# Gate and up of a decode MLP summed with the contraction block outermost, and the last block of W_up loaded on its own

## The chip, the cores and the metric

The kernel runs on one core of a Trainium2 chip. The metric is the device time of one execution in microseconds (us); medians of several runs are quoted, with the lowest and the highest. The profile's span, counted from the program's first instruction to its last, is about 1.8 us shorter than the time.

## The reference

One decode step for two sequences (B = 2, one token, D = 512): layer norm, attention of 32 heads over a cache of 8192 keys and values of 128 elements, output projection and residual, then a second layer norm and a gated MLP with F = 1376:

```python
h  = x + attention(layernorm(x), k_cache, v_cache, wq, wo)
n  = layernorm(h)
gate = n @ W_gate          # 512 x 1376
up   = n @ W_up            # 512 x 1376
gate = gate * (gate > 0)
h2 = h + (gate * up) @ W_down   # 1376 x 512
```

Nearly all of the 281 MB that have to be read are the key and value caches. W_gate, W_up and W_down are 1376 KB each, and they come last.

## The kernel before

The MLP works on transposed vectors: the weights are the stationary operand of TensorE (loaded into it), and the two tokens are the moving one. `F` is cut into 11 chunks `fc` (ten of 128 and one of 96), the contraction `D` into `KC = 4` blocks of 128.

All weights of the tail lie in one tile `W` and are loaded through SyncE's queue, behind the last values:

```python
load_v(N - 1, CUTS)                                  # the last head group's V, in four parts
for g, w in enumerate((B_W_gate, B_W_up)):           # 1376 KB each
    nc.sync.dma_start(out=wgu[:, g], in_=w.rearrange("(c p) n -> p c n", p=P))
wd_l = misc.tile([P, D], bf16)
blocks = [(f, min(4, NF - f)) for f in range(0, NF, 4)]   # chunks 0-3, 4-7, 8-9
for f, r in blocks:                                  # 512, 512 and 256 KB
    nc.sync.dma_start(out=wd_sb[:, f:f + r, :]..., in_=B_W_down[f * P:(f + r) * P, :]...)
nc.sync.dma_start(out=wd_l[0:LASTW, :], in_=B_W_down[FULL:F, :])   # the last 96 rows
```

The sums of gate and up have the chunk outermost, so each chunk's four contraction blocks follow each other, and the first chunk already needs the last block:

```python
def mlp_in(g, ps):
    for fc in [NF] + list(range(NF)):        # the chunk of 96 first
        for c in range(KC):
            # lhsT: the 128 x 128 (or 128 x 96) weights of block c, chunk fc
            nc.tensor.matmul(out=ps[0:w, fc, :], lhsT=lhsT, rhs=hd[:, c, :],
                             start=(c == 0), stop=(c == KC - 1))
mlp_in(0, gate_ps)
var = variance(hd_f, "ln2")
mlp_in(1, up_ps)
# ... gate = max(gate_ps, 0) * 1/(var + eps); act = gate * up_ps, on VectorE, in two parts each
for fc in range(FC):                          # 44 matmuls, chunk by chunk
    for c in range(KC):
        nc.tensor.matmul(out=y_ps[:, c, :], lhsT=(wd_sb[:, fc] or wd_l)[:, c * P:(c + 1) * P],
                         rhs=act[0:w, fc, :], ...)
# ... y = y_ps + hc, two transposes, two copies, one store
```

The softmax here doesn't subtract the row's maximum and nothing guards it: scores larger than these inputs give would overflow.

## Time and profile before

| | before |
|---|---|
| time, median of 3 | 663.18 us (663.14 to 663.24) |
| span | 661.4 us |
| data read | 281 MB at 425 GB/s, DMA over 90% busy in 39 of 40 slices |
| up's matmuls | 654.24 to 655.95 |
| W_down's matmuls | 656.28 to 657.99 |

The page of before, three of its lines: the span, the busy time of each engine, and what the DMA engines moved.

```profile
span 661.4 us, 4234 instructions
...
PE 296.9 (45%) x1704; PEld 131.9 (20%) x1704; DVE 603.0 (91%) x244; ACT 85.0 (13%) x329; POOL 4.7 (1%) x19
...
DMA packets 10699, 281.32 MB, mean 425 GB/s; under 512 B 980, under 2 KB 1592, under 8 KB 4024
```

VectorE and the DMA engines are both above 90%. For a change at the very end of the kernel these shares say nothing; the end has to be read by itself. The timeline gives it. Its columns are start and length in us, engine, source line, operation, what it writes and reads, the number of instructions merged, and in brackets how long the engine sat idle before and what ended that.

```profile
650.84 1.63 PE L429 MATMUL gate_ps<-hd,W 128*96 128x2 bf16 x44 [0.25 <-DVE hd L415]
...
654.24 1.71 PE L429 MATMUL up_ps<-hd,W 128*96 128x2 bf16 x44 [1.34 <-DMA W<-in_B_W_up_dram]
...
655.99 0.24 DVE L448 TENSOR_TENSOR act<-gate,up_ps 96x2 bf16<-96x2 f32 x2 [2.42 <-PE up_ps L429]
656.28 1.61 PE L455 MATMUL y_ps<-act,W 128*128 128x2 bf16 x40 [0.33 <-DVE act L448]
...
657.75 0.24 PE L455 MATMUL y_ps<-act,wd_l 96*128 96x2 bf16 x4
```

TensorE waits 1.34 us for W_up, then sums up (44 matmuls), VectorE multiplies, and TensorE goes on with W_down. Seen in this way, an earlier start of up would move everything behind it. The view of waits (who waited for whom: total us, times, longest) says the same, and it names no wait of `y_ps` for W_down:

```profile
DVE act L448 <- PE up_ps L429: 2.4, 1, 2.4
...
PE up_ps L429 <- DMA W<-in_B_W_up_dram: 1.3, 1, 1.3
...
PE y_ps L455 <- DVE act L448: 0.3, 1, 0.3
```

The chain of waits, which goes from the last instruction back to whatever released each step, tells another story (start, length, what):

```profile
643.88 12.97 DMA W<-in_B_W_down_dram
...
656.90 0.59 PE y_ps L455 x16
...
657.51 0.49 PE y_ps L455 x12
...
658.03 0.18 DVE y L460
```

The chain does not pass through up at all. The matmuls of W_down's second block start at 656.90, and what released them is the landing of a W_down transfer at 656.85. A start that comes at the earliest moment its data allow can be held by these data even if the waits view lists nothing: each matmul is drawn 165 ns long while its successor starts after 27 ns, so the 0.22 us from matmul 16's start (656.681) to matmul 17's (656.900) leave only some 0.05 us of drawn idle time, and that is not listed.

The windows show the queue draining (in each line: busy time of PE, PEld, DVE, ACT, POOL, then the granted TensorE clock, the share of the DMA engines that is busy, and GB/s):

```profile
655.00:656.00 1.00, 0.95 (x32) 0.89 (x30) 0.01 (x1) 0.00 (x0) 0.00 (x0) 0.50 0.56 203
656.00:657.00 1.00, 0.67 (x19) 0.58 (x19) 0.23 (x2) 0.00 (x0) 0.00 (x0) 0.50 0.23 85
657.00:658.00 1.00, 0.97 (x28) 0.80 (x27) 0.00 (x0) 0.00 (x0) 0.00 (x0) 0.50 0.01 5
```

When a transfer has landed is a matter of its slowest engine. The Trainium skill ("DMA: Bandwidth & Descriptors", section "Why a DMA increments its semaphore by 16 and not by 1") says that a transfer runs on up to 16 DMA engines that finish independently and are counted by the semaphore, and that only the full 16 means that all data has landed. The trace has sixteen updates for each of the transfers below, and they lie up to 3.7 us apart at the end of this kernel. From the trace's records of semaphore updates (us):

```
before                 first engine   last engine
W_gate                       647.21        650.67
W_up                         650.64        654.20
W_down chunks 0-3            651.93        655.47
W_down chunks 4-7            653.21        656.85
W_down chunks 8-9            653.91        657.47
W_down last 96 rows          654.24        657.67
```

### The profile page before, as it was taken

How to read it: one execution, taken by the hardware profiler on the slowest of the kernel's cores; microseconds unless marked ns; L12 is line 12 of the kernel's file. 1: busy time of each engine (PE TensorE's matmuls, PEld its weight loads, DVE VectorE, ACT ScalarE, POOL GpSimd, SP SyncE). 2: the span in 40 equal slices, each digit the busy share in tenths (PEclk: the TensorE clock that was granted, in tenths of full speed). 3: DMA queues.
4: the chain of work that ended last, by engine and by line, in shares of the span. 5: the costliest groups of instructions: out<-in, count | busy, mean ns of one | idle time of the engine just before them, and what ended most of it. 6: DMA issues, size and time to landing. Idle time of an engine off the chain costs nothing.

```text
span 661.4 us, 4234 instructions
## 1 busy us (share of the span) xinstructions
PE 296.9 (45%) x1704; PEld 131.9 (20%) x1704; DVE 603.0 (91%) x244; ACT 85.0 (13%) x329; POOL 4.7 (1%) x19
## 2 busy tenths in 40 slices
PE   3108245090633708254380915637081552844346
PEld 1003112030211303122140301213030120321245
DVE  1698999999999999999999999999989999999991
ACT  2111101111100111110111110111111101111110
POOL 2000000000000000000000000000000000000000
PEclk9757768586775857777595867759586775866755
DMA  9999999999999999999999999999999999999996
GB/s 381 444 444 411 458 398 446 428 449 440 402 439 432 444 416 457 408 434 438 417 460 410 428 455 414 446 424 445 412 434 438 427 458 400 440 422 438 412 409 253
DMA packets 10699, 281.32 MB, mean 425 GB/s; under 512 B 980, under 2 KB 1592, under 8 KB 4024
## 3 DMA queue, kind: packets, MB, share of 16 engines
q1 hardware_dynamic: 10676, 281.06, 99.0%
q8 instruction: 13, 0.21, 0.1%
q14 instruction: 6, 0.05, 0.0%
q10 hardware_dynamic: 4, 0.00, 0.0%
HBM read 281.05 MB, written 0.00 MB: 425 GB/s over the span
## 4 chain that ended last, share of the span: by engine, by line
DVE 45%; DMA 41%; PE 8%; SPq 3%; ACT 2%; issue 1%; DVEq 0%
DMA kv<-in_A_k_cache_dram 34%; DVE kv L209 21%; DVE kv L202 21%; PE o L251 7%; DMA W<-in_A_wo_dram 3%; DVE sc L217 3%; SPq L375 3%; DMA W<-in_B_W_down_dram 2%; DMA wq_sb<-in_A_wq_dram 2%; ACT pm L234 2%; PE qps L164 1%; DVE ou L285 0%; DVE rep L282 0%; PE y_ps L455 0%; PE yt_ps L466 0%
## 5 line engine op out<-in xcount | busy, mean ns | idle before, releaser
L251 PE MATMUL o<-kv,pm 128*16 128x512 bf16 x960 | 250.6, 427 | 320.8 <-DMA kv<-in_A_v_cache_dram 290.6
L202 DVE TENSOR_TENSOR kv<-kv,qrep 128x16384 bf16<-128x16384 bf16 (+2 forms) x33 | 278.1, 8427 | 29.7 <-DMA kv<-in_A_k_cache_dram 29.5
L209 DVE TENSOR_TENSOR kv<-kv 128x8192 bf16<-128x8192 bf16 (+5 forms) x132 | 276.9, 2098 | 4.4
L251 PEld LDWEIGHTS <-pm 128*16 128x16 bf16 x960 | 92.4, 98 | 474.6 <-issue 299.4
L234 ACT ACTIVATE pm<-sc 32x128 bf16<-32x128 f32 (+1 forms) x128 | 61.6, 481 | 425.2 <-DVE sc L217 423.8
L217 DVE TENSOR_REDUCE sc<-kv 128x128 f32<-128x1024 bf16 (+2 forms) x33 | 39.2, 1188 | 3.3
L234 ACT ACTIVATION_READ_ACCUMULATOR pm<-sc 32x1 f32 x128 | 31.8, 248 | 0.0
L261 ACT ACTIVATE osb<-o,turn_of 16x128 f32<-16x128 f32 x60 | 16.6, 347 | 115.1 <-PE o L251 107.9
L275 PE MATMUL rep<-osb,head_of 16*128 16x128 f32 x112 | 17.2, 292 | 7.2 <-ACT osb L261 7.2
L275 PEld LDWEIGHTS rep<-osb,head_of 16*128 16x128 f32 x112 | 14.5, 183 | 14.2 <-ACT osb L261 13.1
L292 PE MATMUL o_b<-pm,kv 128*128 128x4 bf16 x256 | 7.4, 166 | 6.6 <-DMA kv<-in_A_v_cache_dram 6.6
L292 PEld LDWEIGHTS <-kv 128*128 128x128 bf16 x256 | 7.3, 105 | 6.9 <-DMA kv<-in_A_v_cache_dram 6.9
L385 PE MATMUL a_ps<-oc,W 128*128 128x2 bf16 x112 | 3.1, 165 | 12.1 <-DVE oc L313 12.1
L164 PE MATMUL qps<-wq_sb,xnb 128*32 128x512 bf16 x64 | 5.4, 501 | 4.8 <-DMA wq_sb<-in_A_wq_dram 4.8
L385 PEld LDWEIGHTS <-W 128*128 128x128 bf16 x128 | 3.7, 104 | 12.4 <-DMA W<-in_A_wo_dram 7.8
L164 PEld LDWEIGHTS <-xnb 128*32 128x32 bf16 x64 | 2.6, 116 | 7.2 <-issue 5.7
L429 PEld LDWEIGHTS <-W 128*128 128x128 bf16 (+1 forms) x88 | 3.3, 120 | 1.6 <-DMA W<-in_B_W_up_dram 1.4
L170 ACT ACTIVATE qrep<-qps 128x512 bf16<-128x512 f32 x4 | 2.4, 597 | 6.2 <-PE qps L164 6.2
L318 DVE RECIPROCAL zil<-zb 128x4 f32<-128x4 f32 x2 | 0.4, 178 | 2.9 <-PE zb L297 2.9
L137 PE MATMUL x_ps<-ident,x_row 2*128 2x2 bf16 x4 | 0.4, 172 | 5.4 <-DMA x_row<-in_A_x_dram 5.4
L285 DVE TENSOR_REDUCE ou<-rep 128x16 f32<-128x512 f32 (+1 forms) x4 | 2.5, 624 | 0.1
L282 DVE TENSOR_TENSOR rep<-rep,pick 128x512 f32<-128x512 f32 (+1 forms) x4 | 2.5, 626 | 0.0
(82 smaller groups left out, 38.9 us busy)
## 6 DMA issues: line engine op xcount, KB each, us to landing
kv<-in_A_k_cache_dram SPq DMA_DIRECT2D x32, 4096.0 KB, 32.3
kv<-in_A_v_cache_dram SPq DMA_DIRECT2D x3, 4096.0 KB, 25.0
wq_sb<-in_A_wq_dram SPq DMA_DIRECT2D x1, 4096.0 KB, 12.2
W<-in_A_wo_dram SPq DMA_DIRECT2D x1, 3584.0 KB, 21.1
kv<-in_A_v_cache_dram SPq DMA_DIRECT2D x1, 2560.0 KB, 26.0
W<-in_B_W_gate_dram SPq DMA_DIRECT2D x1, 1376.0 KB, 29.5
W<-in_B_W_up_dram SPq DMA_DIRECT2D x1, 1376.0 KB
kv<-in_A_v_cache_dram SPq DMA_DIRECT2D x1, 1024.0 KB
```

The costliest lines, as they stand in the source:

```text
L164: nc.tensor.matmul(out=qps[h * Q:(h + 1) * Q], lhsT=xnb[:, c, b, :], rhs=wq_v[:, c, g:g + QP, h, :], start=(c == 0), stop=(c == KC - 1),)
L202: nc.vector.tensor_tensor(out=kt[:, lo:hi, :], in0=kt[:, lo:hi, :], in1=_view(qrep[:, b, i, :], 0, [[0, w], [1, Dh]]), op=ALU.mult)
L209: nc.vector.tensor_tensor(out=_view(kt, off, [[Dh, w], [1, half]]), in0=_view(kt, off, [[Dh, w], [1, half]]), in1=_view(kt, off + half, [[ ...
L217: nc.vector.tensor_reduce(out=sc[:, 0:w], in_=_view(kt, off, [[Dh, w], [1, 8]]), axis=AXIS.X, op=ALU.add)
L234: nc.scalar.activation(out=pm[ps, lo:hi, h], in_=sc[ps, 0:w], func=ACT.Exp, accum_out=(zm[ps, b, k, i:i + 1] if i < LQ else zl[ps, b, k, h ...
L251: nc.tensor.matmul(out=o, lhsT=pm[:, ts, :].rearrange("p t h -> p (t h)"), rhs=vt[:, ts, :].rearrange("p t d -> p (t d)"), start=(t == 0), ...
L261: nc.scalar.activation(out=osb[:, t, :], in_=o[:, t, :], func=ACT.Copy, scale=turn_of[:, t:t + 1])
L275: nc.tensor.matmul(out=reps[i // HQ][:, i % HQ, :], lhsT=head_of.rearrange("k h m -> k (h m)"), rhs=osb[:, t, :], start=(t == 0), stop=(t ...
L292: nc.tensor.matmul(out=o, lhsT=vt[:, t, :], rhs=pm[:, t, :], start=(t == 0), stop=(t == T - 1))
L375: nc.sync.dma_start(out=wd_sb[:, f:f + r, :].rearrange("p r n -> p (r n)"), in_=B_W_down[f * P:(f + r) * P, :].rearrange("(p r) n -> p (r ...
L385: nc.tensor.matmul(out=a_ps[:, c, :], lhsT=w[:, c * P:(c + 1) * P], rhs=o, start=(first and c == 0), stop=last, skip_group_check=True)
L429: nc.tensor.matmul(out=ps[0:w, fc, :], lhsT=lhsT, rhs=hd[:, c, :], start=(c == 0), stop=(c == KC - 1))
```

## The change

The intent: the first three contraction blocks of W_up can be summed while the fourth is still on its way. For this the sums must have the contraction block outermost, and the fourth block needs a transfer, and so a semaphore, of its own. Since all chunks of one bank of PSUM (the memory that TensorE adds its results up in) are now under way at once, only the very first matmul carries the start flag. The chunk of 96 columns, which came first, is now the last of each block. The Trainium skill ("PSUM — Partial Sum Buffer", section "Terms", the rows on `has_written` and the zero region) says that this flag clears the written marks of the whole bank for the quadrants of 32 partitions that it writes, and that a matmul without it overwrites where the mark is clear and adds where it is set. The comparison with the reference can't tell whether these sums are right.

```diff
-    for g, w in enumerate((B_W_gate, B_W_up)):
-        nc.sync.dma_start(out=wgu[:, g], in_=w.rearrange("(c p) n -> p c n", p=P))
+    for g, w, c0, c1 in ((0, B_W_gate, 0, KC), (1, B_W_up, 0, KC - 1), (1, B_W_up, KC - 1, KC)):
+        nc.sync.dma_start(out=wgu[:, g, c0:c1, :],
+                          in_=w.rearrange("(c p) n -> p c n", p=P)[:, c0:c1, :])
 ...
-    def mlp_in(g, ps):
-        for fc in [NF] + list(range(NF)):
-            w = P if fc < NF else LASTW
-            for c in range(KC):
+    def mlp_in(g, ps, c0, c1):
+        for c in range(c0, c1):
+            for fc in range(FC):
+                w = P if fc < NF else LASTW
 ...
-                                 start=(c == 0), stop=(c == KC - 1))
+                                 start=(c == 0 and fc == 0), stop=(c == KC - 1),
+                                 skip_group_check=True)
 ...
-    mlp_in(0, gate_ps)
+    mlp_in(0, gate_ps, 0, KC)
     var = variance(hd_f, "ln2")
-    mlp_in(1, up_ps)
+    mlp_in(1, up_ps, 0, KC - 1)
+    mlp_in(1, up_ps, KC - 1, KC)
```

## The prediction

> **What bounds the kernel.** The page gives VectorE 91% busy, DMA above 90% in 39 of 40 slices, 425 GB/s over the span; 281 MB have to come in. The end is a queue that drains: over windows of half a microsecond the DMA share is 1.0 until 653.5 us, about 0.65 from 654 to 655.5, 0.2 at 656.5, and 0 from 657.5.
>
> **The stage touched**, by the timeline (us from the start): hd is ready at 650.78; the gate matmuls run 650.84-652.47; TensorE then waits 1.34 us for W_up; the up matmuls run 654.24-655.95 (44, about 37 ns apart); the two products run 655.99-656.23; the W_down matmuls run 656.28-657.99; then y, transposes and store.
>
> **Landings.** A transfer's completion is sixteen updates of a semaphore, one for each DMA engine (the Trainium skill, "DMA: Bandwidth & Descriptors", section "Why a DMA increments its semaphore by 16 and not by 1"). The trace agrees, and shows the engines 3.5 us apart: W_gate 647.21 to 650.67, W_up 650.64 to 654.20, W_down's first block (chunks 0-3) to 655.47, the second (4-7) to 656.85, the third (8, 9) to 657.47, the last rows (wd_l) to 657.67. A waiter gets the sixteenth.
>
> **What the change does.** Gate and up still have 44 matmuls each with the same weights and columns; only the order changes. Gate waits for one transfer as before. For up, the first three contraction blocks get their own completion. The slowest engine took 3.53 us for its share of W_up, so three quarters should land at about 653.3 (estimate: 650.67 + 0.75 x 3.53). 33 matmuls then run 653.35-654.6, and 11 remain when the last block lands at 654.2: up ends at about 655.05 instead of 655.95, the products end at about 655.35 instead of 656.23. **Locally 0.9 us earlier.**
>
> **How much is on the critical path.** Hardly any. W_down's first block lands at 655.47, so matmuls 1-16 may run 655.5-656.1. The second block lands at 656.85, and before it chunk 4 cannot start. In before, the chain of waits has W_down's transfer until 656.85 and the next sixteen matmuls start at 656.90 already; the last twelve start at 657.51, just after the third block's 657.47. So W_down's stream was already at the pace of the landings. The end of y stays at about 658.0; the 0.9 us turn into idle time of TensorE before chunk 4.
>
> **What it adds.** One more transfer: one more completion descriptor on each engine (a 4-byte packet takes 9 ns in the trace) and one issue by SyncE. Completion semaphores go round eight, so each W_down issue waits for one transfer later than now; the last, wd_l, for a part of V at 645.96 (issued at 645.80 now). The 17.9 us that W_down's first issue took will be mostly up's last block's. W_down's data start only from 650.6 on, so an issue 1 us later costs nothing. Landings move by 0.0-0.1 us.
>
> **Predicted time: 663.2 us** (change 0.0, perhaps +0.05), range 662.6 to 663.9. Chances: faster by over 2% 0.01, within 2% 0.98, slower 0.01.
>
> **Right or wrong in the profile.** Right if: up's first matmul near 653.3, up's last near 655.05; a new wait of about 0.7 us of the y_ps matmuls for W_down between chunks 3 and 4; y near 658.0. Wrong if y's matmuls end before 657.8, or if up's first matmul still waits until 654.2, or if W_down lands after 658.
>
> **What would make it wrong.** The landings moving by more than 0.3 us, or drift between chips.

## The result, and the profile after

| | before | after |
|---|---|---|
| time, median of 6 | 663.20 us (663.12 to 663.32) | 663.16 us (663.10 to 663.26) |
| span | 661.4 us | 661.4 us |
| up's first matmul | 654.24 | 653.31 |
| products end | 656.23 | 655.33 |
| first matmul of W_down | 656.28 | 655.55 |
| W_down's second block starts | 656.90 | 656.93 |
| y starts | 658.03 | 658.07 |

The ratio after to before is 0.9999, with a 95% interval from 0.9987 to 1.0012: the same. A ratio here is the mean time of one kernel's fast runs over that of the other's fast runs of the same rounds, so it is not quite the ratio of the medians.

The page of after, the same lines:

```profile
span 661.4 us, 4235 instructions
...
PE 295.7 (45%) x1704; PEld 132.7 (20%) x1704; DVE 603.0 (91%) x244; ACT 84.9 (13%) x329; POOL 4.7 (1%) x19
...
DMA packets 10715, 281.32 MB, mean 425 GB/s; under 512 B 996, under 2 KB 1608, under 8 KB 4040
```

There are sixteen packets more (10715 against 10699), all of them under 512 B (996 against 980), which fits one completion update on each of sixteen engines for the added transfer. The timeline of after:

```profile
650.82 1.71 PE L430 MATMUL gate_ps<-hd,W 128*128 128x2 bf16 x44 [0.25 <-DVE hd L416]
...
653.31 1.75 PE L430 MATMUL up_ps<-hd,W 128*128 128x2 bf16 x44 [0.35 <-DMA W<-in_B_W_up_dram]
...
655.09 0.24 DVE L451 TENSOR_TENSOR act<-gate,up_ps 96x2 bf16<-96x2 f32 x2 [1.46 <-PE up_ps L430]
...
655.55 0.58 PE L458 MATMUL y_ps<-act,W 128*128 128x2 bf16 x16 [0.49 <-DMA W<-in_B_W_down_dram]
...
656.93 0.99 PE L458 MATMUL y_ps<-act,W 128*128 128x2 bf16 x24 [0.80 <-DMA W<-in_B_W_down_dram]
...
657.78 0.24 PE L458 MATMUL y_ps<-act,wd_l 96*128 96x2 bf16 x4
```

Up starts 0.93 us earlier and the products end 0.90 us earlier. Then `y_ps` falls into two pieces: sixteen matmuls from 655.55, and twenty-four from 656.93, released by W_down. The waits view names this now:

```profile
DVE act L451 <- PE up_ps L430: 1.5, 1, 1.5
...
PE y_ps L458 <- DMA W<-in_B_W_down_dram: 1.3, 2, 0.8
...
PE up_ps L430 <- DMA W<-in_B_W_up_dram: 0.3, 1, 0.3
```

The wait for W_up has gone from 1.3 to 0.3 us, and a wait of 1.3 us for W_down has come in its place, 0.8 of it in one piece. The starts of single matmuls show where the saving goes. From the products' end to the first matmul of W_down it is now 0.22 us instead of 0.05, and from matmul 16's start to matmul 17's it is 0.97 us (655.965 to 656.931) instead of 0.22. These two alone take back 0.17 and 0.75 us, that is 0.92 us for a gain of 0.90. The chain of waits is the same as before, 0.03 to 0.04 us later:

```profile
644.27 12.62 DMA W<-in_B_W_down_dram
...
656.93 0.59 PE y_ps L458 x16
...
657.55 0.49 PE y_ps L458 x12
...
658.07 0.18 DVE y L463
```

The queue drains much as before:

```profile
655.00:656.00 1.00, 0.51 (x17) 0.46 (x16) 0.24 (x2) 0.00 (x0) 0.00 (x0) 0.50 0.57 208
656.00:657.00 1.00, 0.20 (x7) 0.12 (x5) 0.00 (x0) 0.00 (x0) 0.00 (x0) 0.50 0.27 100
657.00:658.00 1.00, 0.96 (x28) 0.83 (x28) 0.00 (x0) 0.00 (x0) 0.00 (x0) 0.50 0.03 11
```

The last engine's landings in after are 650.66 (gate), 653.26 (three blocks of W_up), 654.20 (the fourth), 655.50, 656.88, 657.51 and 657.70 (W_down), that is 0.03 to 0.04 us behind before for W_down.

### The profile page after: what moved, and what is told of

The parts are those of the page before. It is cut to its first block, busy times and chain, and to the rows that moved or that the text cites. A ratio compares the mean times of both kernels' runs of the same rounds, so it can differ in the third digit from the quotient of the medians.

```text
span 661.4 us, 4235 instructions
## 1 busy us (share of the span) xinstructions
PE 295.7 (45%) x1704; PEld 132.7 (20%) x1704; DVE 603.0 (91%) x244; ACT 84.9 (13%) x329; POOL 4.7 (1%) x19
## 2 busy tenths in 40 slices
DMA packets 10715, 281.32 MB, mean 425 GB/s; under 512 B 996, under 2 KB 1608, under 8 KB 4040
## 4 chain that ended last, share of the span: by engine, by line
DVE 45%; DMA 41%; PE 8%; SPq 3%; ACT 2%; issue 1%; DVEq 0%
DMA kv<-in_A_k_cache_dram 34%; DVE kv L209 21%; DVE kv L202 21%; PE o L251 7%; DMA W<-in_A_wo_dram 3%; DVE sc L217 3%; SPq L370 3%; DMA W<-in_B_W_down_dram 2%; DMA wq_sb<-in_A_wq_dram 2%; ACT pm L234 2%; PE qps L164 1%; DVE ou L285 0%; SPq L376 0%; DVE rep L282 0%; PE y_ps L458 0%
## 5 line engine op out<-in xcount | busy, mean ns | idle before, releaser
L251 PE MATMUL o<-kv,pm 128*16 128x512 bf16 x960 | 248.1, 424 | 322.4 <-DMA kv<-in_A_v_cache_dram 290.6
L297 PE MATMUL zb<-zl,mean_f 128*128 128x4 f32 x12 | 2.8, 354 | 0.0
L297 PEld LDWEIGHTS zb<-zl,mean_f 128*128 128x128 f32 x12 | 2.8, 329 | 0.0
```

What stands on the lines that cost most here:

```text
L251: nc.tensor.matmul(out=o, lhsT=pm[:, ts, :].rearrange("p t h -> p (t h)"), rhs=vt[:, ts, :].rearrange("p t d -> p (t d)"), start=(t == 0), ...
L297: nc.tensor.matmul(out=zb, lhsT=lhsT, rhs=z[:, k, :], start=(k == 0), stop=(k == 2))
```

## The experiments

Theory: W_down's landings set the end of y. The 0.9 us are saved, and lost again in the wait for them. Rival 1: the change saves nothing that can reach the end, because the new order of matmuls costs as much as the early start gains, or because something after y sets the end. Rival 2: one of the two parts alone (order or split) does all there is to do.

Between the 95% intervals of two ratios (about 0.12% each side, 0.8 us) a difference of 0.9 us is at the edge of what can be told. So kernels that ran in the same rounds on the same chip are compared with each other, by the range of their five runs and by their spans.

### Four kernels without the wait for W_down: the 2 x 2 of order and split

The last product takes its weights from the part of W_o that has been in SBUF (the core's on-chip memory) since 626 us. W_down is loaded as before, and nobody reads it. The result is wrong. It still passed the comparison, so "passed" says little about the MLP in any run here.

```diff
-  lhsT=(wd_sb[:, fc] if fc < NF else wd_l[0:w])[:, c * P:(c + 1) * P],
+  lhsT=wo_sb[0:w, fc // J, fc % J, c * P:(c + 1) * P],
```

`res_before` is the kernel before with this edit, `res_after` the changed kernel. `res_order` is the changed kernel with W_up in one transfer; `res_split` is the kernel before with W_up in two.

> Kernel before, but the last product takes its weights from the part of W_o that has long been in SBUF; W_down is still loaded and nobody reads it (wrong result on purpose). Theory (W_down's landings hide the gain): before was limited by up's end and by W_down's landings at once, so without the landings y ends at about 657.9 and the time is 663.1 us (change 0.0 to -0.1). Rival (the end is set by something after y, or the new order costs what the earlier start gains): 663.2 as well. This run is the base of the other three.

> Changed kernel, last product from resident weights in the same way. Theory: up ends at about 655.05, the W_down-free product runs about 655.35 to 657.05, so the time falls by about 0.9 us against res_before, to 662.3. Rival: no fall, 663.1 to 663.2.

> Resident weights for the last product, new order of the sums (contraction block outermost), W_up in one transfer. Theory: the order alone has nothing to start on before 654.2, up runs 654.24 to 655.95 as in before: 663.1 us, same as res_before. Rival (the order itself makes TensorE faster or slower): up's 44 matmuls take clearly other than 1.7 us.

> Resident weights for the last product, old order of the sums, W_up in two transfers. Theory: three matmuls start at 653.3 and the fourth waits for the last contraction block at 654.2, so up ends at about 655.85 and the gain is 0.1 us: 663.0 to 663.1. Rival (the split alone carries the gain): 662.3.

Measured, five runs each (before in the same rounds: 663.15 us, 662.97 to 663.46):

| | order old | order new |
|---|---|---|
| W_up in one transfer | 662.86 (662.60 to 663.21), span 661.0 | 662.83 (662.63 to 662.98), span 661.1 |
| W_up in two | 662.48 (662.40 to 662.71), span 660.7 | 661.77 (661.55 to 661.91), span 660.1 |

The chain of `res_before`, from W_up's landing on:

```profile
622.53 31.66 DMA W<-in_B_W_up_dram
...
654.23 1.73 PE up_ps L429 x44
...
656.27 1.33 PE y_ps L455 x44
```

and that of `res_after`:

```profile
622.40 30.95 DMA W<-in_B_W_up_dram
...
653.39 1.76 PE up_ps L430 x44
...
655.46 1.33 PE y_ps L458 x44
```

With W_down's landings out of the way the chain runs through W_up and up in both, and the change is worth 1.1 us by the medians and 0.9 by the spans of the profiled runs (0.9 was expected; the runs of `res_before` alone scatter over 0.6 us, so the sizes are rough). The ranges of the two don't touch. So rival 1 falls: nothing after y swallows the gain, and the new order doesn't eat it (up's 44 matmuls take 1.75 us in the new order, 1.71 in the old). Rival 2 falls too: the order alone changes nothing (0.03 us), the split alone gives 0.4, both together 1.1.

Two sizes were missed. First, `res_before` was expected 0.0 to 0.1 us below before and came 0.3 below (span 0.4 below). The 44 matmuls of W_down take 1.31 us when nothing holds them and 1.71 in before. So before was already held by W_down's landings for about 0.4 us, in two holes that the starts of single matmuls show: 656.681 to 656.900 ahead of the second block and 657.321 to 657.511 ahead of the third, where neighbours are 27 ns apart (0.19 + 0.16 us lost). Secondly, the split alone was expected to give 0.1 us and gave 0.3 by the span. The three matmuls that it lets run early are those of the chunk with 96 columns, which comes first in the old order. They start 80 ns apart, while those of the eight chunks after them are 32 ns apart; 3 x 80 ns is 0.24 us. The Trainium skill ("TensorE: Matmul & The Clock Gate", section "Weight-path perf modes — Fast Weight Load (FWL) and DoubleRow") says that the fast weight load is on when the number of weights is 128 and the type is not FP32, and that it is about twice as fast. The trace agrees in kind, with a factor of 2.5 from one start to the next (80 against 32 ns, at the granted clock of 0.50). The 32 ns are for weights that are every fourth element; against W_down's, which lie side by side as the 96 do, it is 80 to 27 ns, a factor of 3.0.

### W_up last in the queue

Here W_down's four transfers are issued ahead of W_gate and W_up, so nothing waits for W_down at the end. The edit leaves what is computed as it is.

```diff
+    <the four loads of W_down>
     for g, w ... in (...):          # W_gate, W_up as in before, or as in the change
         nc.sync.dma_start(out=wgu[...], ...)
-    <the four loads of W_down>
```

> Kernel before with W_down's four transfers issued ahead of W_gate and W_up, so that W_up is the last to land and W_down waits for nobody (right result). Theory: the queue still drains at about 657.7, now with W_up; 44 up matmuls (1.71 us as measured), the products (0.3) and 44 W_down matmuls (1.31 us as in the run with resident weights) follow, y's matmuls end near 661.1 instead of 658.0: 666.2 us, about 3 slower.

> Changed kernel with W_down's four transfers issued ahead of W_gate and W_up (right result). Theory: W_up's first three blocks land at about 656.8, the last at 657.7; 33 matmuls are under way by then, up ends near 658.6, y's matmuls near 660.2: 665.3 us, 0.9 less than uplast_before, so the change pays what it saves locally as soon as W_down is not behind W_up. Rival (the change saves nothing that can reach the end): the same as uplast_before.

Measured: `uplast_before` 666.65 us (666.44 to 666.73), `uplast_after` 665.71 (665.53 to 665.97), before in the same rounds 663.13. Both are slower than before, because up, the products and 44 matmuls of W_down now follow the last landing. The chain of `uplast_before`:

```profile
643.23 14.59 DMA W<-in_B_W_up_dram
...
657.87 1.73 PE up_ps L429 x44
```

and of `uplast_after`:

```profile
643.31 13.73 DMA W<-in_B_W_up_dram
...
657.09 1.75 PE up_ps L430 x44
```

The change is worth 0.94 us in this order of loads, as expected (0.9); both times came 0.4 us above the expectation. Of that, 0.1 to 0.2 us are the landings that up starts on: W_up's at 657.82 where 657.7 was assumed, and its first three blocks' at 657.04 where 656.8 was assumed. Another 0.2 us is that the medians lie that far above the profiled runs, which were the fastest of their five. The rest, about 0.1 us or less, was not traced. The same edit pays fully or not at all, by which transfer comes last.

### A dose of work ahead of up's last sums

If the change has turned 0.9 us into slack, then added work of that size must vanish in the changed kernel and show in the kernel before. Twelve matmuls of 96 columns on W_up's last contraction block, written where nobody reads, are put ahead of up's sums (before) or ahead of the last block's eleven (after). What is computed stays as it is.

```diff
+    dm = ps_s.tile([P, 12, B], f32, tag="st", name="dm")
+    for k in range(12):
+        nc.tensor.matmul(out=dm[0:LASTW, k, :], lhsT=wgu[:, 1, KC - 1, FULL:F],
+                         rhs=hd[:, KC - 1, :], start=True, stop=True)
```

(The first of the two steps that invert the variance was moved ahead of it, since it frees the PSUM buffer.)

> Kernel before with 12 more matmuls of 96 columns (80 ns each in the trace) on W_up's last contraction block, written where nobody reads, ahead of the up sums: up ends 0.96 us later, near 656.9 (right result). Theory: in before the W_down stream has only 0.19 + 0.16 us of waits for landings in it, so about 0.6 of the 0.96 us reaches the end: y's last matmul near 658.6, 663.7 us. Rival (this stage doesn't reach the end at all): 663.15.

> Changed kernel with the same 12 matmuls, ahead of up's last contraction block: up ends near 656.05, the products near 656.35. Theory: the change left 0.8 us of idle time ahead of W_down's second block and 0.2 ahead of the third, so the 0.96 us vanish in it: y's end near 658.0, 663.2 us, and about 0.5 us below dose_before. Rival (the change bought no slack): as much slower as dose_before.

Measured: `dose_before` 663.67 us (663.44 to 663.73), `dose_after` 662.96 (662.78 to 663.10), before in the same rounds 663.20 (663.08 to 663.46). The chain of `dose_before`:

```profile
654.29 1.12 PE dm L440 x12
655.41 1.57 PE up_ps L429 x44
...
657.29 1.32 PE y_ps L459 x44
```

and of `dose_after`:

```profile
644.02 12.80 DMA W<-in_B_W_down_dram
...
656.87 0.59 PE y_ps L462 x16
...
657.47 0.49 PE y_ps L462 x12
```

In before, 0.5 (by the medians) to 0.6 (by the spans, 662.0 against 661.4) of the 0.96 us reach the end, and the chain has moved over to W_up. In the changed kernel they vanish (span 661.3, against 661.4 without the dose), and the chain is W_down's, as without the dose. The time even came 0.2 us below the 663.2 that were expected; the changed kernel without the dose did not run in these rounds, and W_down's landings were 0.06 to 0.09 us earlier than in after, so a difference of this size is not explained further. The two differ by 0.7 us, with ranges that don't touch. So the gain is still there, as slack on TensorE ahead of W_down's second block: with the dose that wait shrinks to what it was in before (0.22 us from matmul 16's start to matmul 17's).

### Can the last landing come earlier? A probe and a try that failed

Since W_down's landings set the end, the next question is why the DMA engines are 3.5 us apart. The probe loads the last 96 rows of W_down as 4, 8 and 84 rows. By the Trainium skill ("DMA: Bandwidth & Descriptors", section "Why a DMA increments its semaphore by 16 and not by 1", its part "How many engines (k)") a transfer runs on the largest number k of engines, at most 16, that divides its number of rows, and on the lowest-numbered ones of the core: here 4, 8 and 14. The trace gives no engine's number.

```diff
-    nc.sync.dma_start(out=wd_l[0:LASTW, :], in_=B_W_down[FULL:F, :])
+    for lo, hi in ((0, 4), (4, 12), (12, LASTW)):
+        nc.sync.dma_start(out=wd_l[lo:hi, :], in_=B_W_down[FULL + lo:FULL + hi, :])
```

> Kernel before, with the last 96 rows of W_down loaded as 4, 8 and 84 rows[...]. No theory of the change is at stake: it tells which engines are the late ones at the end (landings spread over 3.3 us). If the late three are among the last two or eight engines, the k=8 transfer has no landing later than 2.4 us after its first. Time about 663.2.

Measured: 663.31 us in its single run, state unknown. The trace has 4, 8 and 14 landings for the three transfers, as the page says; which engines these are it doesn't show. The transfer just ahead of them has four late engines, 3.0 to 3.5 us behind the first; the next is 2.3 behind. The k = 4 transfer has no landing after 656.54, the k = 8 one has one late landing (657.52), the k = 14 one has four (657.31 to 657.77). So, if the numbering is as the page says, one late engine is among 4 to 7 and three are among 8 to 13. The expectation (none in the first eight) was missed.

`bal7` is the changed kernel with W_down's third block loaded as 119 and 9 rows, to keep it off most of the late engines. By the same rule it then runs on 7 and on 9 engines, and the trace has 7 and 9 landings.

```diff
-            out=wd_sb[:, f:f + r, :]..., in_=...)
+        for lo, hi in (((0, P),) if r == 4 else ((0, 119), (119, P))):
+            out=wd_sb[lo:hi, f:f + r, :]..., in_=...[lo:hi])
```

> Changed kernel with the third block of W_down (256 KB) loaded as 119 and 9 rows[...] (right result).[...] If the late one is engine 7, the late engines are spared about 16 KB each and W_down's last landing moves from 657.7 to about 657.3, the time to 662.8. If the late one is among 4 to 6, it gets more and the last landing moves to about 658.3, the time to 663.8. Either way the time follows the last landing (theory).

Measured: 664.70 us (664.28 to 665.15) against 663.20, ratio 1.0021 with an interval from 1.0009 to 1.0034. The last landing moved to 658.41, the second block's from 656.88 to 658.14 and the first block's from 655.50 to 656.69. The timeline of `bal7` has the two pieces of W_down's matmuls at these landings:

```profile
656.74 0.59 PE L459 MATMUL y_ps<-act,W 128*128 128x2 bf16 x16 [1.55 <-DMA W<-in_B_W_down_dram]
...
658.19 0.80 PE L459 MATMUL y_ps<-act,W 128*128 128x2 bf16 x24 [0.87 <-DMA W<-in_B_W_down_dram]
```

The time follows the landings once more, which is what the theory says. But neither of the expected times (662.8 and 663.8) came, and their reasoning doesn't explain it: the first block lands 1.2 us later, and even W_up's last block 0.3 us later (654.51), although both stand ahead of the odd transfer in the queue. Why that is stays open, and so does whether the late engine among 4 to 7 is engine 7. No experiment here gave a correct version that beats both kernels.

## Why the prediction was right, point by point

- **Time.** Predicted 663.2 us with no change; measured 663.16 against 663.20. Right.
- **W_up's first three blocks land at about 653.3.** Measured 653.26. The estimate (650.67 plus three quarters of the slowest engine's 3.53 us, 653.32) was good to 0.06 us.
- **Up ends near 655.05, products near 655.35.** Measured 655.06 and 655.33. Right, 0.9 us earlier.
- **W_down's stream is at the pace of the landings, so the gain becomes idle time of TensorE ahead of chunk 4.** Right: the wait of `y_ps` for W_down was predicted at 0.7 us between chunks 3 and 4, and the waits view has 0.8. The runs with resident weights (1.1 us gained) and with the dose (0.7 us apart) show that these landings hide the gain.
- **The added transfer costs 0.0 to 0.1 us.** W_down's landings are 0.03 to 0.04 us later than in before. The same landings vary by about 0.1 us from one profile to the next (657.47 in before and 657.52 in `dose_before` for the third block, 657.51 in after and 657.43 in `dose_after`), so this can't be told from chance.
- **The long issue.** SyncE's 17.9 us of issuing W_down's first block became 16.85 us of issuing W_up's last block, and the last transfer was issued at 645.96 instead of 645.80, as predicted. It did no harm.
- **"44, about 37 ns apart."** This was a mean over unlike things. The matmuls are 80 ns apart for the chunk of 96 columns, 32 for the eight chunks of gate and up whose weights are every fourth element, and 27 for their last two chunks (every second element) and for W_down (contiguous). The prediction's result didn't hang on it, but it hid that before was held by the landings for 0.35 us and not just barely. Two expectations of the experiments were wrong by 0.2 to 0.3 us for this reason.

## What to carry to other kernels

When the last inputs of a kernel are still landing while it works on them, write down for each the landing of its last engine and ask what may start then; a stage that is made to finish early gains nothing if the next one waits for a later landing. A wait that is just met does not appear among the waits, only in the chain and in holes between the starts of single instructions, so a list of waits cannot prove that data are early enough. To tell a gain that was lost from one that was never there, take the suspected wait away (here by reading weights that have long been there), or add a known dose of work and see whether it vanishes. And a comparison that passes with wrong weights in a stage is no test of that stage.

## What the Trainium skill lacked or had wrong

- "DMA: Bandwidth & Descriptors" says that the engines of a transfer finish independently, but not how far they drift in a long queue that never empties. In before the first transfer's sixteen landings were 0.38 us apart and those of the tail 3.4 to 3.7 us, and a waiter gets the latest.
- No page gives a figure for what an instruction packet costs the data that share its DMA engine. The trace of before has thirteen of 16 KB that took 0.99 to 1.12 us each. The spread of the landings rose from 0.38 to 1.70 us between the transfers that landed at 51.7 and at 62.8 us, and the only such packet up to then ran at 55.9 us. That they cause the drift was not tested.
- "DMA: Bandwidth & Descriptors", section "Latency and other measured facts", says that engines 7 and 15 are usually slower than the others (with a guess at the cause that holds for another way of issuing). In the probe's trace, if the engines are numbered as the page says, three of the four late engines are among 8 to 13 and none is 14 or 15.
- "TensorE: Matmul & The Clock Gate", section on the fast weight load: it gives about 2 as the factor, and here it was 2.5 to 3.0 for 96 against 128 columns (80 against 32 or 27 ns from one matmul to the next with two moving columns). Weights that are every fourth element cost 5 ns more than contiguous ones or every second element (32 against 27 ns), for which that section gives no cost.
